# Products of a tile of ones on TensorE in the opening of an attention and double gated-MLP kernel

## The chip, the cores and the metric

The kernel runs on one core of one Trainium2 chip. The metric is the device time of one execution in microseconds (us); several executions of a kernel are timed and their median is compared. One further execution is taken with the hardware profiler, and all rows below come from that one.

## What is computed

Attention over pooled keys and values, then two gated MLPs, all in float32:

```
k_p, v_p = mean of k, v over groups of 8 positions        # 576 -> 72 positions, 4 batches, 8 heads, 64 wide
attn = softmax(q @ k_p.T / 8);  x = attn @ v_p            # x: 2304 tokens x 512
xn = x / sqrt(mean(x*x) + 1e-6) * rms_g
x  = (silu(xn @ w_gate) * (xn @ w_val)) @ w_out           # 512 -> 1536 -> 512
y  = ((x @ w_a) * (x @ w_b)) @ w_out2                     # 512 -> 1536 -> 512
```

The weights arrive as 64-bit floats, so each 128x512 block is loaded as raw words and converted on the chip.

## The kernel before, in words

The work goes through the tokens in tiles of 512, 256, 512, 512 and 512 for the first MLP (`TILES1`), then through the second MLP in slices of 768. Attention is computed in units of 256 tokens, each of two halves of 128. Only the opening matters here: the attention of the first two units, the normalisation of their rows, and the first tile of the first MLP beside the conversion of the weights.

The steps of a unit `u` are small functions. `score_steps` (L288) makes `Au.0` to `Au.9`. Of them `Au.0` and `Au.5` transpose a half of q on TensorE (L298) and copy it out on ScalarE (L307), which frees the buffer of q and lets the next load of q be issued on the SP queue (L283). `Au.1`, `Au.2`, `Au.6` and `Au.7` multiply it with the pooled keys (L318), and VectorE takes the maximum and subtracts it (L327, L328). `Au.3`, `Au.4`, `Au.8` and `Au.9` are the exponential on ScalarE and the division by the row sums. `value_steps` (L358) makes `Vu.0` to `Vu.7`: transposes of the weights of attention (L367), their copies (L374), products with the values (L420), sums of squares with a matrix of ones (L434), a narrow reciprocal square root on VectorE in Newton steps (L478 to L493), a diagonal matrix of the roots (L464), the spread of these roots over all partitions by a product with ones (`spread`, L472), and the scaling (L529). For units 0 and 1 each float32 product shows as two instructions in the trace.

What comes before the scores: k is loaded and pooled on VectorE and GpSimd, transposed (`t0`, L210), and copied into `KB` by ScalarE for one half and VectorE for the other (L220, L222). `ones` (L118) is a 128x128 tile filled by VectorE at the start.

The order of the opening is a list of tokens written by hand, `FIRST` (L32 to L48). `first_tile` hands each to `token` (L763), which runs the named step. After an `@` stand the tags of the PSUM banks that the step takes, in place of the common two. A token with `-` or `=` is put behind the last step without a prefix, on ScalarE, VectorE and GpSimd (`run`, L703); on TensorE no instruction is held in this way, since no step without a prefix is remembered for it. Within that, the framework's scheduler lays out each engine's queue at compile time, from the order of the tokens and from its own model of when an operand is ready. On the chip each queue is worked off in that fixed order, and semaphores make an instruction wait for its operands. `g0a`, `v0a` and so on are halves of the products of the first MLP (L799), `o0` the product with its output weights (L670), `c` the conversion of a block of weights (L589, L590 on ScalarE, L596, L599 on VectorE, L606 on GpSimd), `s0.0` the split of a block into a high and a low part (L620, L621).

```
FIRST = """
=k0 -A0.0@att =k1 l -k2! k3 -l t0@att =A0.1@acc1 A0.2@att w0 =A0.5@acc0 =A0.6@acc3 =A0.7@acc3
-w1 A0.3 =A0.4 w2 t1 =A0.8 A1.0@att A1.1@acc0 A0.9! =c l =A1.2@v -V0.0@acc0 A1.5@acc2 -A1.3
...
```

Of the kernel before, what the change touches and what calls it, by code (L numbers as in the profile page):

```python
# [8 lines left out]
F32 = mybir.dt.float32  # L9
# [8 lines left out]
P = 128  # L18
# [11 lines left out]


FIRST = """  # L32
=k0 -A0.0@att =k1 l -k2! k3 -l t0@att =A0.1@acc1 A0.2@att w0 =A0.5@acc0 =A0.6@acc3 =A0.7@acc3
-w1 A0.3 =A0.4 w2 t1 =A0.8 A1.0@att A1.1@acc0 A0.9! =c l =A1.2@v -V0.0@acc0 A1.5@acc2 -A1.3
-V0.1@acc1 c A1.6@acc3 s0.0 -V0.2@acc0,v A1.4! -V0.3@g,acc0 =A1.7@acc1 A1.8 A1.9 V0.4@acc2,att
=V0.5@att -c =V1.0@acc0 =V0.6 =V0.7@v =V1.1@g -x0! -g0a V1.2@att,acc3 =V1.3@acc2,acc1 c =g0b
-V1.4@acc0,att =l V1.5@acc2 =V1.6 =V1.7@acc0 s0.1! =c =x1 -a0 s1.0 =v0a =v0b -c =h0 =o0 -g1a
-g1b -s1.1! =c L0 -a1 A2.0 -g2a v1a =L1 -g2b p0 =p1! v1b =c s2.0! h1 =c =a2 =c g3a =c v2a =v2b
-h2 =c g3b =o1 a3 =p2 =o2 -v3a =v3b -s2.1 -h3 g4a g4b p3! -c a4 -v4a s3.0 =c -p4 -v4b s3.1! =c
=o3 =g5a =p5! =c =h4 c -c s4.0! -g5b -c -a5 s4.1! v5a -s5.0 v5b -h5 -g6a -o4 -g6b a6 -p6 -c  # L40
=v6a p7 -s5.1 =v6b -A2.1 -g7a -c =g7b -h6 =c =M0 -c =A2.2 =c -A2.3 =s6.1! =s6.0! -a7 o5 -c v7a
=c =A2.4 v7b s7.0! -h7 -g8a -g8b =a8 -o6 s7.1! c =v8a A2.5 c =s8.0 =p8 v8b =g9a -V2.0 g9b -h8
-a9 -o7 v9a =g10a -s9.0 v9b -c =s8.1 -h9 =c =V2.1 =o8 -V2.2 g10b =s9.1! -a10 -c V2.3 =v10a
-V2.4 -c v10b s10.0 g11a -g11b -h10 =a11 =V2.5 =c -s10.1 =c =o9 -g12a =c -v11a s11.0 =A3.0
=g12b -v11b h11 =a12 -V2.6 -v12a =s12.0 -g13a c -o10 A3.1 -v12b -o11 =g13b -s11.1 -s12.1!
=A3.2 -A3.3 =M1 -h12 a13 -v13a -V2.7 -v13b =o12 -h13 =A3.4 =o13 =A3.5
""".split()
SECOND = """  # L48
A4.0 =r0 -r1 r2 -r3 r4 -r5 V3.0 r7 =r6 =r8 -V3.1 =V3.2 N0 =V3.3 A4.1 -N1
# [14 lines left out]
def attention_moe_moe2(  # L64
# [14 lines left out]
    nc = tc.nc  # L79
# [29 lines left out]
    ps = first.enter_context(tc.tile_pool(name="ps", bufs=1, space=bass.MemoryType.PSUM))  # L109
# [7 lines left out]
    ones = const.tile([P, P], F32R, tag="ones", name="ones")  # L117
# [24 lines left out]
    def att_bank(name, tag=None):  # L142
        if tag is not None:
            pass
        else:
            tag = boot["banks"].pop(0) if boot["banks"] else "att"
        return ps.tile([P, 512], F32, tag=tag, name=name, bufs=2 if tag == "att" else 1)
# [210 lines left out]
    def value_steps(u, dest):  # L358
        t0, n = u * UNIT, UNIT
# [109 lines left out]
        def spread():  # L469
            if "diag" in box:  # L470
                bank = att_bank(f"rb_{u}")
                nc.tensor.matmul(  # L472
                    bank[:, :n], ones.bitcast(F32), box["diag"], start=True, stop=True
                )
                box["r"] = bank[:, :n]
# [50 lines left out]
        def scale():  # L526
            xf = dest()
            spread()
            nc.vector.tensor_mul(xf, xf, box["r"].unsqueeze(1).to_broadcast([P, KD, n]))  # L529
# [191 lines left out]
    PE = mybir.EngineType.PE  # L721
    HELD = (PE, mybir.EngineType.Activation, mybir.EngineType.DVE, mybir.EngineType.Pool)
    names = {}

    def name(key, steps):
        for i, st in enumerate(steps):
            names[f"{key}{i}"] = st

    x0 = []

    def split_half(h):
# [17 lines left out]
    name("x", [lambda h=h: split_half(h) for h in range(2)])  # L749
    name("N", loads[3])  # L750
    names["."] = lambda: None
    for u in range(5):
        name(f"A{u}.", A[u])
        name(f"V{u}.", V[u])
# [560 lines left out]
```

## Time and profile before

| | us |
|---|---|
| median of 3 executions | 1023.58 (1022.65 to 1023.66) |
| the profiled execution, its own time | 1024.57 |
| its span, first to last instruction | 1022.8 |
| mean granted TensorE clock over the span | 0.985 of full |

How to read it: times in the rows are microseconds from the start of the span, unless marked ns. PE is TensorE's matmul, PEld its weight load, DVE VectorE, ACT ScalarE, POOL GpSimd, SP the queue that issues the transfers. L298 is line 298 of the kernel before. A group of matmuls that follow each other closely has a start and a length; neighbouring matmuls overlap in the record, so the distance between starts tells the rate, and the length of one tells its latency. The granted clock is the share of full speed that the throttle gave TensorE: 1.00 is 2.4 GHz and 0.50 is 1.2 GHz.

### The profile page before, as it was taken

What the parts mean: (1) busy time and instruction counts of PE and PEld (TensorE: products, weight loads), DVE (VectorE), ACT (ScalarE), POOL (GpSimd) and SP (SyncE); (2) the same over time, 40 slices, a digit from 0 to 9 for tenths busy, and PEclk for the clock granted to TensorE, in tenths of its full rate; (3) what the DMA queues carried; (4) which work ended last, traced back from release to release, by engine and by line L of the source; (5) the groups of instructions that cost most, each with busy time, mean ns of one, the idle gap of its engine ahead of it and who ended that gap; (6) DMA issues with size and microseconds to landing.
All of it is one profiled execution on the core that took longest, in us unless ns stands there. A gap on an engine that the chain in (4) does not pass through costs nothing.

```text
span 1022.8 us, 13568 instructions
## 1 busy us (share of the span) xinstructions
PE 980.8 (96%) x4920; PEld 845.7 (83%) x4920; DVE 612.5 (60%) x966; ACT 451.7 (44%) x848; POOL 399.6 (39%) x324
## 2 busy tenths in 40 slices
PE   4988999999999989999999999999999999999998
PEld 3776676788888877888788899999999999888886
DVE  6898966775634764463628759766776665222221
ACT  3845662454535445444445445444444434321211
POOL 6476672533343433343348611533344333310000
PEclk9889999999999999999999999999999999999999
DMA  8556544320100001000111133443444345643431
GB/s 228 156 175 195 176 141 107 113 70 1 42 8 14 1 6 57 1 1 1 42 44 60 42 115 128 125 160 119 148 146 127 126 137 183 193 136 124 140 115 67
DMA packets 82802, 101.55 MB, mean 99 GB/s; under 512 B 24112, under 2 KB 63024, under 8 KB 82736
## 3 DMA queue, kind: packets, MB, share of 16 engines
q1 hardware_dynamic: 82736, 100.69, 31.7%
q8 instruction: 39, 0.64, 0.3%
q14 instruction: 27, 0.22, 0.1%
HBM read 73.93 MB, written 26.74 MB: 98 GB/s over the span
## 4 chain that ended last, share of the span: by engine, by line
PE 81%; DVE 12%; DMA 3%; issue 2%; ACT 1%; SPq 0%; DVEq 0%; ACTq 0%
PE o L1120 15%; PE X L1019 14%; PE v L649 10%; PE g L649 10%; PE acc L662 9%; PE Y L1019 7%; PE acc L670 4%; PE Z L1019 3%; PE xT L399 2%; PE g L799 2%; PE v L799 2%; PE sc L318 1%; DVE wf L596 1%; DVE wf L599 1%; DMA kv<-in_k_dram 1%
## 5 line engine op out<-in xcount | busy, mean ns | idle before, releaser
L621 POOL TENSOR_TENSOR wl<-wf,wh 128x512 fp32r<-128x512 f32 x144 | 193.6, 1351 | 242.6 <-ACT wh L620 230.3
L620 ACT CAST wh<-wf 128x512 fp32r<-128x512 f32 x156 | 94.9, 618 | 77.9 <-PE v L649 31.8
L1098 DVE TENSOR_TENSOR hl<-hf,hh 128x768 fp32r<-128x768 f32 x36 | 34.3, 958 | 95.5 <-ACT hh L1097 95.4
L1120 PE MATMUL o<-woh,hl 128*128 128x512 f32 x216 | 85.8, 397 | 0.0
L1120 PE MATMUL o<-woh,hh 128*128 128x512 f32 x216 | 85.0, 393 | 0.0
L1120 PE MATMUL o<-wol,hh 128*128 128x512 f32 x216 | 84.7, 392 | 0.0
L606 POOL TENSOR_TENSOR w<-w,st 128x512 int32<-128x512 int32 x24 | 31.9, 1328 | 115.8 <-DVE w L599 114.6
L649 PE MATMUL v<-xh,wl 128*128 128x512 f32 (+1 forms) x192 | 72.7, 379 | 1.8 <-DVE ht L1241 1.8
L649 PE MATMUL g<-xh,wl 128*128 128x512 f32 (+1 forms) x192 | 73.0, 380 | 0.0
L649 PE MATMUL g<-xh,wh 128*128 128x512 f32 (+1 forms) x192 | 70.2, 366 | 0.0
L649 PE MATMUL g<-xl,wh 128*128 128x512 f32 (+1 forms) x192 | 70.2, 366 | 0.0
L649 PE MATMUL v<-xl,wh 128*128 128x512 f32 (+1 forms) x192 | 69.9, 364 | 0.0
L649 PE MATMUL v<-xh,wh 128*128 128x512 f32 (+1 forms) x192 | 69.7, 363 | 0.0
L1097 ACT CAST hh<-hf 128x768 fp32r<-128x768 f32 x36 | 29.8, 834 | 89.8 <-PE o L1120 83.0
L670 PE MATMUL acc<-ht,wf 128*128 128x256 f32 (+1 forms) x208 | 67.5, 466 | 1.2 <-DVE ht L813 0.7
L606 POOL TENSOR_TENSOR wf<-wf,st 128x512 int32<-128x512 int32 x36 | 52.9, 1476 | 39.0 <-DVE wf L599 17.3
L1241 DVE TENSOR_TENSOR ht<-ht,v 128x512 f32<-128x512 f32 (+1 forms) x48 | 29.6, 617 | 64.1 <-PE v L649 60.0
L662 PE MATMUL acc<-hh,wl 128*128 128x512 f32 x144 | 57.5, 399 | 3.8 <-ACT hh L1250 3.8
L1233 ACT ACTIVATE ht<-g 128x512 f32<-128x512 f32 (+1 forms) x48 | 26.1, 544 | 77.8 <-PE g L649 71.7
L662 PE MATMUL acc<-hl,wh 128*128 128x512 f32 x144 | 57.0, 396 | 0.1
L1027 ACT COPY p<-X 128x384 f32<-128x384 f32 x36 | 17.2, 478 | 90.2 <-PE X L1019 90.2
L662 PE MATMUL acc<-hh,wh 128*128 128x512 f32 x144 | 56.8, 394 | 0.0
(208 smaller groups left out, 2713.2 us busy)
## 6 DMA issues: line engine op xcount, KB each, us to landing
hf<-h SPq DMA_DIRECT2D x36, 384.0 KB
st<-in_moe_w_out_dram SPq DMA_DIRECT2D x24, 512.0 KB
h<-u SPq DMA_DIRECT2D x36, 192.0 KB
h<-p SPq DMA_DIRECT2D x36, 192.0 KB
st<-in_moe_w_gate_dram SPq DMA_DIRECT2D x12, 512.0 KB
st<-in_moe_w_val_dram SPq DMA_DIRECT2D x12, 512.0 KB
st<-in_moe_w_a_dram SPq DMA_DIRECT2D x12, 512.0 KB
st<-in_moe_w_b_dram SPq DMA_DIRECT2D x12, 512.0 KB
```

Source lines behind the costliest of these rows:

```text
L606: nc.gpsimd.tensor_tensor(out=bits, in0=bits, in1=low, op=ALU.add)
L620: nc.scalar.copy(wh, wf[ph, f, i])
L621: (nc.vector if boot["alt"] else nc.gpsimd).tensor_sub(wl, wf[ph, f, i], wh.bitcast(F32))
L649: nc.tensor.matmul(bank[:, :n], w[:, c, :], x[:, c, cols], start=(i == 0), stop=(i == 3 * KD - 1),)
L662: nc.tensor.matmul(accs[c][:, cols], w[:, c, :], x[:, :n], start=(f == 0 and i == 0 and cols.start == 0), stop=(f == NF - 1 and i == 2),)
L670: nc.tensor.matmul(accs[c][:, cols], wf[0, f, 2][:, c, :], ht[:, :cols.stop - cols.start], start=(f == 0 and cols.start == 0), stop=(f == ...
L799: nc.tensor.matmul(bank[:, :n], w[:, c, :], x[:, c, cols], start=(c == 0 and i == 0), stop=(c == KD - 1 and i == len(terms) - 1),)
L1019: nc.tensor.matmul(dst[:, :HALF], w[:, c0 + c, :], x[:, c, :], start=(start and i == 0), stop=(stop and i == 5), skip_group_check=True,)
L1097: nc.scalar.copy(hh, hf)
L1098: nc.vector.tensor_sub(hl, hf, hh.bitcast(F32))
L1120: nc.tensor.matmul(accs[i], x[:, sub], y, start=(f == 0 and j == 0), stop=(f == NF - 1 and j == 2),)
L1241: nc.vector.tensor_mul(ht[:, :m], ht[:, :m], vb[:, :m])
```

## The change

Forty-eight products are added, of `ones` with `ones` repeated four times, 128x512 each, in the type fp32r (one instruction and one weight load each). Nothing reads what they write. Each has an ordering edge behind the last TensorE instruction traced before it, with no semaphore; nothing is put behind them by such an edge. They stand in three places:

- `z`, the first token: 24 products, with no TensorE instruction ahead of them.
- `y`: 2 products each behind `A0.0`, `A0.1`, `A0.2`, `A0.5`, `A0.6`, `A0.7`, `A1.0` and `A1.1`, 16 in all. `z` and `y` write one bank with the tag `g`, whose next user is the step `V0.3`.
- `spread` of units 0 and 1: 4 products each, into the bank that the spread itself then writes.

No step of the kernel is removed or moved in the list, and no transfer is added. The diff, with the rest of `FIRST`, which is only wrapped anew, left out:

```
+z =k0 -A0.0@att y =k1 l -k2! k3 -l t0@att =A0.1@acc1 y A0.2@att y w0 =A0.5@acc0 y =A0.6@acc3 y
+=A0.7@acc3 y -w1 A0.3 =A0.4 w2 t1 =A0.8 A1.0@att y A1.1@acc0 y A0.9! =c l =A1.2@v -V0.0@acc0
...
                 bank = att_bank(f"rb_{u}")
+                if u < 2:
+                    keep_busy(4, bank)
                 nc.tensor.matmul(
                     bank[:, :n], ones.bitcast(F32), box["diag"], start=True, stop=True
                 )
...
+    busy = {}
+
+    def keep_busy(count, bank=None):
+
+        before = [i for i in nc.cur_bb.bb.instructions if i.engine == PE]
+        if bank is None:
+            if not busy:
+                busy["bank"] = ps.tile([P, 512], F32, tag="g", name="busy")
+            bank = busy["bank"]
+        for _ in range(count):
+            ins = nc.tensor.matmul(
+                bank, ones, ones.unsqueeze(1).to_broadcast([P, 4, P]), start=True, stop=True
+            ).ins
+            if before:
+                tc.add_manual_dep(
+                    ins, before[-1].name,
+                    mybir.DependencyInfo(mybir.DependencyClass.NoSync, mybir.DependencyReason.DATA),
+                    reason="behind",
+                )
...
+    names["z"] = lambda: keep_busy(24)
+    names["y"] = lambda: keep_busy(2)
```

## Rows read from the trace of the kernel before

**Rows 1.** The page, busy time and share of the span of each engine.

```profile
PE 980.8 (96%) x4920; PEld 845.7 (83%) x4920; DVE 612.5 (60%) x966; ACT 451.7 (44%) x848; POOL 399.6 (39%) x324
```

**Rows 2.** Chain that ended last, 10 to 36 us: start, us, what.

```profile
13.06 2.27 PE sc L318 x8
...
15.81 0.73 DVE e L328 x2
...
24.33 0.90 PE eT L367 x3
25.23 0.96 PE sc L318 x4
26.19 0.43 PE eT L367 x2
26.62 1.71 PE xT L420 x4
...
29.12 0.86 PE xT L420 x4
...
34.14 0.47 PE sq L434 x4
```

**Rows 3.** TensorE in order of time, opening: start, length, [idle before, what ended it].

```profile
10.44 1.09 PE L298 MATMUL qT<-ident,q 128*128 128x128 f32 x4 [10.44 <-DMA q<-in_q_dram]
11.32 0.69 PE L210 MATMUL kT<-ident,kp 72*128 72x72 f32 x4
...
13.06 2.75 PE L318 MATMUL sc<-KB,qTs 128*128 128x144 f32 x12 [0.20 <-DVE KB L222]
...
17.55 0.73 PE L318 MATMUL sc<-KB,qTs 128*128 128x144 f32 x4 [1.04 <-DVE e L328]
...
40.75 0.60 PE L298 MATMUL qT<-ident,q 128*128 128x128 f32 x4
```

**Rows 4.** Busy us (instructions) of PE, PEld, DVE, ACT, POOL; granted clock; DMA share, GB/s.

```profile
22.00:28.80 6.80, 5.77 (x21) 5.03 (x22) 6.47 (x15) 3.15 (x9) 4.43 (x5) 0.50 0.73 227
42.40:49.30 6.90, 5.53 (x23) 4.92 (x23) 5.73 (x15) 6.03 (x12) 2.53 (x3) 0.51 0.76 201
56.10:62.90 6.80, 6.29 (x27) 5.81 (x27) 5.23 (x5) 1.52 (x3) 5.55 (x6) 0.50 0.61 195
10.40:15.00 4.60, 4.36 (x20) 3.99 (x21) 1.92 (x4) 1.53 (x3) 2.31 (x4) 1.00 1.11 318
...
30.00:35.00 5.00, 5.00 (x35) 4.01 (x36) 4.34 (x10) 4.57 (x13) 0.94 (x2) 1.00 0.19 63
...
70.00:80.00 10.00, 8.57 (x44) 7.11 (x43) 9.93 (x13) 5.99 (x10) 8.63 (x7) 1.00 0.77 247
```

**Rows 5.** TensorE in order of time: fp32r products at either clock.

```profile
47.02 0.41 PE L799 MATMUL g<-xh,wh 128*128 128x256 f32 x1
47.23 0.41 PE L799 MATMUL g<-xl,wh 128*128 128x256 f32 x1
...
300.02 0.39 PE L649 MATMUL v<-xh,wh 128*128 128x512 f32 x1
300.24 0.39 PE L649 MATMUL v<-xl,wh 128*128 128x512 f32 x1
```

**Rows 6.** VectorE in order of time: the fill of ones.

```profile
0.88 0.17 DVE L118 MEMSET ones<- 128x128 f32 x1 [0.88 <-PEq L1293]
```

**Rows 7.** TensorE's waits, 32 to 62 us: us in total, times, longest.

```profile
PE rb L472 <- DVE dg L464: 0.9, 1, 0.9
...
PE rb L472 <- DVE dg L464: 2.0, 1, 2.0
PE kT L210 <- DVE kp L189: 1.1, 1, 1.1
```

**Rows 8.** VectorE's waits, 45 to 64 us.

```profile
DVE ht L813 <- PE v L799: 1.6, 1, 1.6
```

More of the change, by code (lines that the diff above doesn't have):

```diff
@@ L32 @@
 FIRST = """
[L33 to L44, printed above, removed]
@@ L45 @@
-=g12b -v11b h11 =a12 -V2.6 -v12a =s12.0 -g13a c -o10 A3.1 -v12b -o11 =g13b -s11.1 -s12.1!
-=A3.2 -A3.3 =M1 -h12 a13 -v13a -V2.7 -v13b =o12 -h13 =A3.4 =o13 =A3.5
+z =k0 -A0.0@att y =k1 l -k2! k3 -l t0@att =A0.1@acc1 y A0.2@att y w0 =A0.5@acc0 y =A0.6@acc3 y
+=A0.7@acc3 y -w1 A0.3 =A0.4 w2 t1 =A0.8 A1.0@att y A1.1@acc0 y A0.9! =c l =A1.2@v -V0.0@acc0
+A1.5@acc2 -A1.3 -V0.1@acc1 c A1.6@acc3 s0.0 -V0.2@acc0,v A1.4! -V0.3@g,acc0 =A1.7@acc1 A1.8
+A1.9 V0.4@acc2,att =V0.5@att -c =V1.0@acc0 =V0.6 =V0.7@v =V1.1@g -x0! -g0a V1.2@att,acc3
@@ new lines @@
+=V1.3@acc2,acc1 c =g0b -V1.4@acc0,att =l V1.5@acc2 =V1.6 =V1.7@acc0 s0.1! =c =x1 -a0 s1.0 =v0a
+=v0b -c =h0 =o0 -g1a -g1b -s1.1! =c L0 -a1 A2.0 -g2a v1a =L1 -g2b p0 =p1! v1b =c s2.0! h1 =c
+=a2 =c g3a =c v2a =v2b -h2 =c g3b =o1 a3 =p2 =o2 -v3a =v3b -s2.1 -h3 g4a g4b p3! -c a4 -v4a
+s3.0 =c -p4 -v4b s3.1! =c =o3 =g5a =p5! =c =h4 c -c s4.0! -g5b -c -a5 s4.1! v5a -s5.0 v5b -h5
+-g6a -o4 -g6b a6 -p6 -c =v6a p7 -s5.1 =v6b -A2.1 -g7a -c =g7b -h6 =c =M0 -c =A2.2 =c -A2.3
+=s6.1! =s6.0! -a7 o5 -c v7a =c =A2.4 v7b s7.0! -h7 -g8a -g8b =a8 -o6 s7.1! c =v8a A2.5 c =s8.0
@@ L47 @@
+=p8 v8b =g9a -V2.0 g9b -h8 -a9 -o7 v9a =g10a -s9.0 v9b -c =s8.1 -h9 =c =V2.1 =o8 -V2.2 g10b
+=s9.1! -a10 -c V2.3 =v10a -V2.4 -c v10b s10.0 g11a -g11b -h10 =a11 =V2.5 =c -s10.1 =c =o9
+-g12a =c -v11a s11.0 =A3.0 =g12b -v11b h11 =a12 -V2.6 -v12a =s12.0 -g13a c -o10 A3.1 -v12b
+-o11 =g13b -s11.1 -s12.1! =A3.2 -A3.3 =M1 -h12 a13 -v13a -V2.7 -v13b =o12 -h13 =A3.4 =o13
+=A3.5
 """.split()
```

## The prediction

> **What bounds the kernel now.** I first read the page's busy shares. TensorE is busy for 96% of the span and no other engine for more than 60% [rows 1], so over most of the kernel only TensorE's work or its speed counts. The opening is where it is not fed, and there I read the chain of waits, then TensorE in order of time, then the stretches with their clock.
>
> The chain runs through TensorE in two places. The first is 13.06 to 15.33, eight score products that VectorE waits for; the second is 24.33 to 34.6, transposes, scores and value products one behind the other with hardly a gap [rows 2]. In between, from 15.8 on, it is mostly VectorE. TensorE does nothing before 10.44, when q has landed [rows 3].
>
> Then the speed. Three stretches of 6.8 to 6.9 us run at a granted clock of 0.50, which is 1.2 GHz: 22.0 to 28.8, 42.4 to 49.3 and 56.1 to 62.9. The table gives 1.00 for 10.4 to 15 [rows 4]. The lengths of the instructions speak against that last figure: four transposes of q take 1.09 us at 10.44 and 0.60 at 40.75, and the first twelve score products take 2.75 where a group of four takes 0.73 at 17.55 [rows 3]. So I take the first burst to have run at the lower of the two clocks, up to about 15, with nothing recorded before the first change. The Trainium skill, "TensorE: Matmul & The Clock Gate" (What's actually happening), says that the throttled state is where the engine starts and that activity releases it, and its caveat under Seeing it yourself says not to trust single records of the clock; the lengths agree with it, the column does not. By the column the first part of the sum below would be a small loss, not a gain; that is a rival.
>
> **The price of one product.** At full clock fp32r products of 512 columns start 0.22 us apart, say 0.23 with its neighbours. At the low clock those of 256 columns start 0.21 apart [rows 5], so one of 512 takes about 0.43, an estimate by twice the columns.
>
> **z, 24 products.** They can start when the ones are filled, at 1.05 [rows 6], and wait for nothing else. The low clock lasted 6.8 us in the stretches that the table shows [rows 4] and about 4.6 in the first burst. If it rises 4.6 to 6.8 us after z starts, 11 to 16 products run at 0.43 and the rest at 0.23, and z ends at 1.05 + 11 x 0.43 + 13 x 0.23 = 8.8 or at 1.05 + 16 x 0.43 + 8 x 0.23 = 9.8. Both lie before 10.44: z costs nothing, its cover being the wait for q. Without a rise it ends at 1.05 + 24 x 0.43 = 11.4, 0.9 late.
>
> **y, and the first scores at full clock.** The four transposes of q fall from 1.09 to 0.60, so their copy starts 0.49 earlier. Two products, 0.46, then stand ahead of the transposes of k. Those started at 11.32 and ended at 12.01 [rows 3]; now they start at 10.88 + 0.46 = 11.34, and with half their spacing end at about 11.75. KB's two copies move with that, and the scores start about 0.3 earlier, at 12.76. Eight of them took 2.27 [rows 2]. Now the first four take 0.56 at 0.14 a start, a pair of 0.46 stands behind them, and the second four are done 0.73 after their start, as at 17.55: 12.76 + 0.56 + 0.46 + 0.73 = 14.5 instead of 15.33. So VectorE's two subtractions at 15.81 [rows 2] come about **0.8** earlier. The other six pairs stand behind a transpose or a score whose reader is ScalarE or VectorE; VectorE is the fuller engine there, so I price them at nothing, and at 0.46 each for those that would stand on the chain (two at most, 0.9). The pairs hold no queue but TensorE's. On SP the loads of q that wait for a transpose are issued up to 0.5 earlier, and nothing is issued later than before except behind a delayed transpose, by up to 0.46.
>
> Of the 0.8 I carry **0.7** to 24.33. The bounds are 0, if transfers or GpSimd set the pace there, and 0.8; with the two pairs on the chain after all, -0.2 is left.
>
> **22.0 to 28.8.** TensorE is busy for 5.77 of 6.8 us here [rows 4]. The four links on the chain from 24.33 take 0.90, 0.96, 0.43 and 1.71, in all 4.00 [rows 2]. At full clock the value products take 0.86, as they do at 29.12 [rows 2]. Scores at 0.14 a start take 0.56 for four, and five transposes at 0.11 take 0.55. That is 1.97 in place of 4.00, so at most 2.0 is to be had. ScalarE must copy the transposes in between, and from 30 to 35 it is busy for 4.57 of 5 us [rows 4], so it is late next. I take **1.5**. Whether the clock holds is unknown: the pairs end behind the first score of the third half, near 19, and the thin stretch after that has only what it had. The bounds are 0, if the clock falls where it fell, and 2.0. I take the upper side, since the stretch before 22 gets four products, 0.9 us of work, and what follows moves forward.
>
> **The fours ahead of the spreads.** They depend on nothing but their place behind the last TensorE instruction traced, so I expect the scheduler to put them well ahead of the spread: in the dense run near 34.5 for unit 0, after the sums of squares near 43.5 for unit 1. Each four costs 4 x 0.23 = 0.9, or 1.7 at the low clock. Their cover is TensorE's idle time of 0.9 ahead of the first spread, and of 1.1 at the transpose of k near 45 ahead of the 2.0 of the second spread [rows 7]. I price them at 0, with bounds of +0.9 (the cover moved away) and, if they keep the clock up in the last low stretch, a gain of up to 1.6: that is what VectorE waits for one value product, v, in that stretch [rows 8]. In 42.4 to 49.3 ScalarE and VectorE are busy for 6.03 and 5.73 of 6.9 us [rows 4], so a faster TensorE there brings nothing.
>
> **The sum.** -0.7 - 1.5 + 0 = -2.2. After 64 us everything follows from conversions and transfers that were themselves released by work of the opening, so I let the 2.2 stand until the end. The profiled execution took 1024.57, 1.0 above the median of 1023.58; it would become 1022.4, and the median **1021.4**. A measurement of this kernel can tell about 0.2% from no change, here 2.05 us, so 1021.53 and 1025.63 are the limits of "the same"; the forecast lies just past the lower one.
>
> **The rivals.**
> - *The last low stretch goes too.* The 1.6 comes on top: 1019.8. For it speak the fours; against it that they may stand 10 us before that stretch. Chance 0.16.
> - *The clock falls near 22 as before, or, as the column has it, the first burst was already fast.* In the first case only the 0.7 is won: 1022.9. In the second the two pairs on the chain cost 0.9 and the 1.5 is won: 1023.0. The long transposes speak against the second. Chance 0.21, of which 0.04 for the column.
> - *It is taken up.* VectorE is busy for 9.93 of 10 us from 70 to 80 [rows 4], where the weights are converted as they land, and what comes earlier waits there; or the scheduler sinks the products to places where they hold nothing up and keep nothing fast, which is the change not doing what it says. 1023.6, chance 0.08.
> - *Slower.* The products stand strictly in TensorE's queue. If the clock is low at 10.44 all the same, because z left it low or because the idle time between z and q let it fall, then the pairs ahead of the first two score groups cost 0.86 each in place of 0.46 and nothing gets faster: 0.9 ahead of the transpose of k, 0.9 behind the second transpose of q and 0.9 between the groups, 2.6 in all: 1026.2. It decides at the first transposes: a length over 0.4 us each. For it speaks that 0.6 to 1.6 us of idle time lie ahead of 10.44; against it that an idle 1.04 us ahead of 17.55 [rows 3] was followed by fast scores. Chance 0.15.
>
> **How the numbers follow.** The forecast has 0.40, with a range of its own from 1020.5 to 1022.7. Of it 0.31 lies below 1021.53; with the first rival's 0.16 that makes faster 0.47. The rest of it, 0.09, with 0.21 and 0.08 makes the same 0.38. Slower is 0.15. The range reaches from 1019.0 (both low stretches gone, less what ScalarE holds back) to 1025.6; beyond it lie most of the slower case and a rest below, 2 in 10.
>
> **What would show it.** Right: the first four transposes take about 0.6 us, the first maximum comes near 13.5 and the subtractions near 15.0; the granted clock is 1.00 from 22 to 28.8; the last sums of squares of unit 0 end near 32.4 instead of 34.6. Wrong: z ends after q has landed; the transposes still take over 1 us; the clock falls near 21 or 25; the spreads start later against the diagonals; or the gain seen at 34 is gone by 90, where VectorE and the loads set the pace.

## The result and the profile after

The kernel became slower. Its median is **1037.19 us** (4 executions, 1036.27 to 1038.78) against 1023.62 for the kernel before beside it: a ratio of 1.0131, interval 1.0114 to 1.0148, some 13.6 us. The profiled execution took 1038.09. The forecast was 1021.4 with a range up to 1025.6, so both its sign and its range were wrong.

The span of that execution is 1036.4 us, against 1022.8 before. The page after, busy time and share of the span of each engine:

```profile
PE 993.1 (96%) x4968; PEld 853.3 (82%) x4968; DVE 618.7 (60%) x966; ACT 452.0 (44%) x848; POOL 401.1 (39%) x324
```

The shares are those of [rows 1]: nothing here shows where 13.6 us went. The table of stretches of after does. (Line numbers differ from kernel to kernel; the names of the tiles do not.) Its columns are the stretch and its length, then busy time and instructions by engine, the granted clock, the transfers' share and GB/s:

```profile
10.40:15.00 4.60, 4.14 (x20) 3.54 (x21) 2.10 (x4) 1.57 (x3) 2.21 (x3) 0.64 1.11 304
...
40.00:50.00 10.00, 6.04 (x27) 4.01 (x25) 8.51 (x17) 5.07 (x13) 3.93 (x3) 0.79 0.74 212
...
60.00:70.00 10.00, 3.40 (x12) 2.63 (x13) 8.51 (x11) 0.00 (x0) 7.68 (x8) 0.64 0.48 147
```

From 40 to 50 TensorE is busy for 6.04 us of 10 and from 60 to 70 for 3.40, while VectorE is busy for 8.51 in both. TensorE of after in order of time, from those rows that answer to [rows 3] and [rows 7] and the new products (brackets: idle time ahead, and what ended it):

```profile
1.10 7.49 PE L742 MATMUL busy<-ones 128*128 128x512 f32 x24 [1.10 <-DVE ones L119]
10.66 0.63 PE L299 MATMUL qT<-ident,q 128*128 128x128 f32 x4 [2.07 <-POOL kp L184]
...
37.23 1.17 PE L742 MATMUL rb<-ones 128*128 128x512 f32 x4
...
47.26 0.36 PE L211 MATMUL kT<-ident,kp 72*128 72x72 f32 x1 [3.15 <-DVE by L495]
47.95 1.22 PE L475 MATMUL rb<-dg,ones 128*128 128x256 f32 x2 [0.34 <-DVE dg L465]
...
52.23 2.05 PE L742 MATMUL rb<-ones 128*128 128x512 f32 x4
...
68.25 1.22 PE L475 MATMUL rb<-dg,ones 128*128 128x256 f32 x2 [5.05 <-DVE dg L465]
```

The products ahead of q do what was forecast: they end at 8.59 and the first four transposes of q take 0.63, not 1.09 [rows 3]. But the spread of unit 0 comes at 47.95, and that of unit 1 at 68.25; the kernel before has them at 40.21 and 54.73. Ahead of both TensorE waits for VectorE, 3.15 us (at the k transpose just in front of the spread) and 5.05 us. That k transpose stood over 5 us behind the first spread before, at 45.83 for 40.21.

VectorE of after between unit 0's sums and its diagonals (dg), and one step of unit 1's root:

```profile
37.34 0.15 DVE L481 TENSOR_SCALAR ba<-sq 128x4 f32<-128x4 f32 x1
37.45 0.69 DVE L602 SCALAR_TENSOR_TENSOR wf<-st,wf 128x512 int32<-128x512 int32 x1
...
38.13 0.42 DVE L599 TENSOR_SCALAR wf<-wf 128x512 int32<-128x512 int32 x1
38.47 1.27 DVE L488 TENSOR_SCALAR br<-br 128x4 int32<-128x4 int32 x1
39.65 0.68 DVE L602 SCALAR_TENSOR_TENSOR wf<-st,wf 128x512 int32<-128x512 int32 x1
...
40.33 0.41 DVE L599 TENSOR_SCALAR wf<-wf 128x512 int32<-128x512 int32 x1
40.66 1.25 DVE L495 TENSOR_TENSOR by<-by,ba 128x4 f32<-128x4 f32 x1
41.83 0.68 DVE L602 SCALAR_TENSOR_TENSOR wf<-st,wf 128x512 int32<-128x512 int32 x1
...
42.81 1.15 DVE L495 TENSOR_TENSOR by<-by,ba 128x4 f32<-128x4 f32 x1
43.99 1.19 DVE L496 SCALAR_TENSOR_TENSOR br<-by,br 128x4 f32<-128x4 f32 x1
45.10 1.01 DVE L190 TENSOR_REDUCE kp<-kv 72x64 f32<-72x512 f32 x1
...
46.11 1.01 DVE L190 TENSOR_REDUCE kp<-kv 72x64 f32<-72x512 f32 x1
...
47.42 0.48 DVE L465 TENSOR_SCALAR dg<-ident,br 128x128 f32<-128x128 f32 x2
...
61.42 3.96 DVE L495 TENSOR_TENSOR by<-by,ba 128x4 f32<-128x4 f32 x1
...
67.63 0.56 DVE L465 TENSOR_SCALAR dg<-ident,br 128x128 f32<-128x128 f32 x2
```

The same part of VectorE in the kernel before:

```profile
34.63 0.16 DVE L478 TENSOR_SCALAR ba<-sq 128x4 f32<-128x4 f32 x1
34.83 1.11 DVE L481 TENSOR_SCALAR br<-ba 128x4 int32<-128x4 int32 x1
...
36.65 0.42 DVE L596 TENSOR_SCALAR wf<-wf 128x512 int32<-128x512 int32 x1
...
37.11 0.69 DVE L599 SCALAR_TENSOR_TENSOR wf<-st,wf 128x512 int32<-128x512 int32 x1
...
38.10 1.14 DVE L491 TENSOR_TENSOR by<-br 128x4 f32<-128x4 f32 x1
...
39.67 0.48 DVE L464 TENSOR_SCALAR dg<-ident,br 128x128 f32<-128x128 f32 x2
```

From the first step of the root to dg it is 10.08 us after and 5.04 before. The 5.04 more can be counted from one start to the next: five instructions of conversions stand among the steps where two did (2.5 for 0.95, so 1.5), two reduces of k (1.9), and four steps hold VectorE for over 1.1 where two did, though their usual length is 0.16 (4.6 for 2.3, so 2.3); the short steps, eight for ten, take 0.7 less. Why a step on 128x4 elements takes over a microsecond, GpSimd of after shows:

```profile
38.28 1.43 POOL L609 TENSOR_TENSOR wf<-wf,st 128x512 int32<-128x512 int32 x1 [6.26 <-DVE br L484]
40.46 1.42 POOL L609 TENSOR_TENSOR wf<-wf,st 128x512 int32<-128x512 int32 x1 [0.76 <-DVE by L494]
42.64 1.29 POOL L609 TENSOR_TENSOR wf<-wf,st 128x512 int32<-128x512 int32 x1 [0.76 <-ACT wh L623]
43.90 1.26 POOL L624 TENSOR_TENSOR wl<-wf,wh 128x512 fp32r<-128x512 f32 x1
...
62.88 2.48 POOL L624 TENSOR_TENSOR wl<-wf,wh 128x512 fp32r<-128x512 f32 x2
```

Each long step ends with a GpSimd instruction: 39.74 and 39.71, 41.91 and 41.88, 43.96 and 43.93, 45.18 and 45.16; the one of 3.96 ends at 65.38, the two of 2.48 at 65.36. A conversion put among the root's steps therefore costs twice in this trace: its own time, and the GpSimd work behind it (L609 for three of the steps, the split L624 for the fourth), which a small step waits out; the step of 3.96 waits out several in a row. The Trainium skill, "SBUF — State Buffer" (SBUF: two separate sides), says that VectorE and GpSimd share one pair of ports under an exclusive lock, which a VectorE instruction needs if it has two inputs in SBUF or runs in a two-port mode, and that the loser waits for the whole instruction; these ends agree with it.

So the account along the path is: unit 0's sums 2.7 late (37.34 for 34.63), its root 5.0 longer, 1.1 more up to unit 1's sums (52.41 for 43.57), unit 1's root 4.95 longer (15.22 from ba to dg for 10.27): 13.8 at unit 1's diagonals and 13.5 at its spread, where the spans differ by 13.6 at the end. The activations of the first MLP carry it on: 12.0 late at 65, 14.9 at 200, 13.0 from 258.

No line of the change touches VectorE. The two programs compared instruction by instruction, with the 48 products left out, differ in the **order** of their queues: at 201 places of TensorE's (within the first 316), 124 of VectorE's, 65 of ScalarE's, 18 of GpSimd's and 14 of SP's. Whatever stands behind is in the same order.

### The profile page after: what moved, and what is told of

It reads as the page before. It is cut to its first block, busy times and chain, and to the rows that moved or that the text cites. A ratio compares the mean times of both kernels' runs of the same rounds, so it can differ in the third digit from the quotient of the medians.

```text
span 1036.4 us, 13661 instructions
## 1 busy us (share of the span) xinstructions
PE 993.1 (96%) x4968; PEld 853.3 (82%) x4968; DVE 618.7 (60%) x966; ACT 452.0 (44%) x848; POOL 401.1 (39%) x324
## 4 chain that ended last, share of the span: by engine, by line
PE 79%; DVE 12%; DMA 4%; issue 2%; ACT 2%; POOL 1%; SPq 0%; DVEq 0%; ACTq 0%; POOLq 0%
PE o L1145 14%; PE X L1044 13%; PE v L652 10%; PE g L652 10%; PE acc L665 9%; PE Y L1044 6%; PE acc L673 3%; PE Z L1044 3%; PE xT L400 2%; PE g L824 2%; PE sc L319 1%; PE v L824 1%; DMA kv<-in_k_dram 1%; DVE wf L599 1%; DVE kp L190 1%
## 5 line engine op out<-in xcount | busy, mean ns | idle before, releaser
L624 POOL TENSOR_TENSOR wl<-wf,wh 128x512 fp32r<-128x512 f32 x144 | 192.7, 1346 | 244.3 <-ACT wh L623 232.2
L609 POOL TENSOR_TENSOR w<-w,st 128x512 int32<-128x512 int32 x24 | 31.9, 1328 | 116.0 <-DVE w L602 114.8
L609 POOL TENSOR_TENSOR wf<-wf,st 128x512 int32<-128x512 int32 x36 | 55.4, 1546 | 48.7 <-DVE wf L602 26.2
```

Source lines behind the costliest of these rows:

```text
L609: nc.gpsimd.tensor_tensor(out=bits, in0=bits, in1=low, op=ALU.add)
L624: (nc.vector if boot["alt"] else nc.gpsimd).tensor_sub(wl, wf[ph, f, i], wh.bitcast(F32))
```

## The experiments

To part the products from the order, a table writes out each engine's queue and ties every instruction to the one ahead of it. A number counts an engine's instructions in the order in which the kernel's code makes them. Of each queue only the stretch in question is shown, cut at both ends, and words stand for whole queues. On VectorE 44 to 57 is unit 0's root from ba to dg, 63 to 76 unit 1's, 61 and 62, 79 and 80, 83 and 84 are pairs of a conversion (43 is the second half of another), 89 and 90 reduces of k, 58 and 77 the scaling of x by a spread. On TensorE 64 and 101 are the spreads, 276 the k transpose.

```diff
+ORDER = {"PE": [...], "DVE": [...], "Activation": [...], "Pool": [...], "SP": [...]}
...
+    for e, seq in want.items():
+        for p, c in zip(seq, seq[1:]):
+            tc.add_manual_dep(lists[e][c], lists[e][p].name, NO_SYNC, reason="order")
```

**The order alone.** No products; the kernel before with all five queues in after's order.

```diff
-# DVE, as scheduled: 44, 45, 46, 47, 48, 49, 61, 50, 62, 51, 52, 53, 54, 55, 56, 57, 79, 80, 58
+"DVE": 44, 43, 45, 61, 46, 62, 47, 79, 48, 80, 49, 50, 51, 52, 89, 53, 90, 54, 55, 56, 57, 58
```

> The kernel before, without any product, with the queues of all five engines put in the order that they have in the changed kernel (edges without a semaphore between neighbours, over the first 316 TensorE, 172 VectorE, 134 ScalarE, 81 GpSimd and 51 SP instructions, where the two differ). Theory 'order' (the products made the scheduler lay out other queues, and these cost the time): 1035 to 1039, about what the changed kernel takes. Theory 'products' (their own time on TensorE and the clock cost it): 1022.5 to 1025. Half and half: near 1030.

Measured: 1036.79 (4 executions), ratio 1.0119 [1.0095, 1.0142]. The products are not needed for the loss; it is the order. Its root of unit 0 takes 10.09 us (36.51 to 46.60) and its second spread comes at 67.30, nearly after's figures.

**The products alone.** All 48, with the queues of before.

```diff
+    nc.tensor.matmul(bank, ones, ones.unsqueeze(1).to_broadcast([P, 4, P]), start=True, stop=True)
+"DVE": 44, 45, 46, 47, 48, 49, 61, 50, 62, 51, 52, 53, 54, 55, 56, 57, 79, 80, 58
```

> The changed kernel with all 48 products, with every other instruction of all five engines in the order of the kernel before. Theory 'order': at most 1025, and if the prediction's sum holds once the order is kept, 1020.5 to 1022.5. Theory 'products': 1035 to 1039.

Measured: 1022.86 (10 executions), ratio 0.9983 [0.9965, 1.0002]. The same kernel once more, in more rounds:

> The kernel with all 48 products and everything else in before's order, once more (1022.86 over 10 runs before, ratio 0.9983 [0.9965, 1.0002]). If the products by themselves are worth what the clock of the first 50 us gives back, 1.1 to 1.3 at the activations between 50 and 120 us in the first run: 1021.5 to 1023.5, with the interval below 1. If the fall of the clock at later waits eats it: the interval holds 1.

Measured: 1023.91 (12 executions), ratio 0.9999 [0.9989, 1.0010]. By themselves the products bring nothing that can be measured, though the clock is what the forecast hoped for and more. The stretches of the products alone:

```profile
22.00:28.80 6.80, 4.79 (x31) 3.83 (x30) 6.73 (x14) 4.45 (x12) 4.82 (x5) 1.00 0.85 249
...
40.00:50.00 10.00, 7.68 (x52) 6.51 (x51) 9.15 (x19) 9.27 (x17) 4.00 (x3) 1.00 0.64 191
```

VectorE of the products alone, with one row of TensorE, says where the gain of the front ends:

```profile
15.27 0.81 DVE L339 TENSOR_TENSOR e<-sc,m 128x288 f32<-128x288 f32 x2
...
21.64 0.84 DVE L351 TENSOR_SCALAR sum<-sum 128x8 f32<-128x8 f32 x1
22.39 0.41 DVE L609 TENSOR_SCALAR wf<-wf 128x512 int32<-128x512 int32 x1
...
28.24 0.20 DVE L352 RECIPROCAL sum<-sum 128x8 f32<-128x8 f32 x1
...
33.10 1.18 PE L752 MATMUL rb<-ones 128*128 128x512 f32 x4
33.34 0.69 DVE L612 SCALAR_TENSOR_TENSOR wf<-st,wf 128x512 int32<-128x512 int32 x1
34.77 0.16 DVE L491 TENSOR_SCALAR ba<-sq 128x4 f32<-128x4 f32 x1 [0.74 <-PE sq L445]
```

In before the same steps stand at 15.73, 22.38, 22.45, 28.30 and 34.63. The gain is 0.46 at the subtractions and 0.74 at the sum's scaling (L351); there that step, usually 0.16, takes 0.84 beside a GpSimd instruction, and from the conversion on the two kernels run alike up to 28.3, at full clock in the one and at half in the other. VectorE is busy for 6.73 of 6.8 us. Behind 28.3 the products alone are 0.46 ahead once more (the conversion at 33.34 stands at 33.80 in before), and the four products ahead of unit 0's spread take that back: they stand at 33.10 for 1.18, in front of the last sums of squares, and VectorE waits 0.74 for those.

**Groups of products**, all in before's order. The first alone:

```diff
-"z =k0 -A0.0@att y =k1 l -k2! k3 -l t0@att =A0.1@acc1 y A0.2@att y w0 ..."
+"z =k0 -A0.0@att =k1 l -k2! k3 -l t0@att =A0.1@acc1 A0.2@att w0 ..."
-                if u < 2:
-                    keep_busy(4, bank)
```

> Only the 24 products of z, with every other instruction in the order of the kernel before. Theory 'order': 1022 to 1024, a gain of up to 0.8 if the clock is still up when q lands. Theory 'products': between 1024 and 1030, since half of the products are left.

Measured: 1026.27 (10), ratio 1.0016 [1.0002, 1.0031], outside the 1022 to 1024 of the theory of the order: 24 products in before's order ran 1.7 over before, where all 48 ran 1.7 under it. Why was not found. The same without the table, in the order that the scheduler gives:

```diff
-ORDER = {"PE": [...], "DVE": [...], "Activation": [...], "Pool": [...], "SP": [...]}
```

> Only the 24 products of z, laid out by the scheduler as it likes; some 20 places on TensorE, 14 on VectorE and 6 on ScalarE then differ from the kernel before. Theory 'order': its distance to the run with z in the old order is what these places cost; it may have either sign, within 4. Theory 'products': the same time as that run, within 0.5.

Measured: 1027.44 (10), ratio 1.0021 [1.0004, 1.0037]; the intervals of the two overlap. Even with only 24 products ahead of q the scheduler lays out other queues; unit 0's sums come at 35.57 and its spread at 41.25. The first two groups without the fours:

```diff
-                if u < 2:
-                    keep_busy(4, bank)
```

> The products ahead of the first q and those behind the first two units' score steps, but not the fours ahead of the spreads; every other instruction in before's order. With all 48 it was 1022.86, with those ahead of the first q alone 1026.27, before 1024.6. If the groups behind the scores hold the clock past 25 us: low clock of 21.3 to 28 in the run with the first group alone goes, and unit 0's sums end near 34.7 as with all 48. If the fours ahead of the spreads hold it past 40: here the clock falls again in 40 to 50 and the time is 1024 to 1026. If the fours do nothing: as with all 48, 1021.5 to 1024, and the spread itself about 0.4 earlier.

Measured: 1023.76 (10), ratio 1.0004 [0.9989, 1.0019]. The last two without the first:

```diff
-z =k0 -A0.0@att y =k1 l -k2! k3 -l t0@att =A0.1@acc1 y A0.2@att y w0
+=k0 -A0.0@att y =k1 l -k2! k3 -l t0@att =A0.1@acc1 y A0.2@att y w0
```

> The products behind the scores and ahead of the spreads, without those ahead of the first q; everything else in before's order. In the run with the first group alone (1026.27) the q transposes went from 1.09 to 0.63 and the activations came 0.6 to 1.0 earlier up to 120 us, but the time was longer. If the first group is worth its 0.5 to 0.7 and no more: 0.5 to 0.7 over the run beside it with all 48. If the first group costs something (as it seemed alone): 1 or more under the run beside it. If it does nothing: within 0.4 of it.

Measured: 1027.52 (8), ratio 1.0033 [1.0019, 1.0046]. Here the clock, from 22 to 28.8 and 40 to 50, with the first group alone:

```profile
22.00:28.80 6.80, 5.16 (x22) 4.47 (x21) 6.51 (x13) 3.60 (x10) 4.89 (x5) 0.58 0.75 220
...
40.00:50.00 10.00, 8.62 (x42) 7.79 (x40) 8.72 (x18) 8.59 (x16) 4.05 (x3) 0.56 0.65 187
```

and with the first two:

```profile
22.00:28.80 6.80, 5.07 (x32) 3.87 (x31) 6.77 (x16) 5.14 (x13) 4.40 (x5) 1.00 0.89 246
...
40.00:50.00 10.00, 8.47 (x43) 7.47 (x44) 9.15 (x19) 8.49 (x16) 3.99 (x3) 0.66 0.64 192
```

The pairs behind the scores keep 22 to 28.8 at full clock (0.58, then 1.00), and the fours keep 40 to 50 (0.66, then 1.00 above). Each group does to the clock what it is for. The times don't follow: unit 0's sums come at 33.88 with the first group alone, at the low clock, at 34.38 with two groups and at 34.77 with all. None of the three things expected of the last run was measured: it is 3.6 slower than the kernel with all 48 beside it, where the first group was to be worth 0.7 at most. Why was not settled: its profiled execution took 1024.43, its fastest, while the others took up to 1029.99. The first group alone ran 1.7 over before and the kernel without it 3.1 over, so these runs give no price for a single group.

**Which part of the order.** After's order up to unit 0's sums and before's behind them, then the mirror:

```diff
+"DVE": [after's order of 0 to 43 and 78] + [before's order of the rest]
```

> No products. Each queue has after's order for what stands, in before, ahead of the first step of unit 0's inverse root (on TensorE up to unit 0's last sum of squares), and before's order for all that follows. All of after's order was 1036.79, before 1023.8 to 1024.6. Theory A (the cost lies behind the sums, in the cut-up roots, the spreads behind other work and the products of the second layer): 1024 to 1027, the front only 1 to 2 late at unit 0's sums (36.0 against 34.6 in the run with all of after's order). Theory B (the front sets it: unit 1's softmax and transposes come later, and what follows waits): 1031 or more.

Measured: 1026.73 (10), ratio 1.0026 [1.0017, 1.0036]; the second spread at 57.27.

```diff
+"DVE": [before's order of 0 to 43 and 78] + [after's order of the rest]
```

> No products. The mirror of the run before: before's order up to unit 0's sums, after's order for all that follows. Theory A: 1033 to 1037, the spread of unit 0 behind 44 and that of unit 1 behind 64. Theory B: 1025 to 1029. If the two parts add up, the excesses of both runs over before sum to 12.

Measured: 1034.78 (4), ratio 1.0098 [1.0079, 1.0116]; the spreads at 44.34 and 64.69. Over before (1024.14) that is 2.6 and 10.6, in all 13.2 where the whole order costs 12: most of the cost lies behind the sums. Now by engines: TensorE's and VectorE's queues of after with the other three of before, and the mirror:

```diff
+"PE": after, "DVE": after, "Activation": before, "Pool": before, "SP": before
```

> No products. TensorE's and VectorE's queues in after's order, ScalarE's, GpSimd's and SP's in before's. All of after's order 1036.79, before 1024. Theory A (the two queues that hold the roots, the spreads and the products carry it): 1034 to 1037. Theory B (the DMA issues and the conversions on ScalarE and GpSimd that moved carry it, through late weights): 1024 to 1028.

Measured: 1039.19 (4), ratio 1.0154 [1.0139, 1.0168], 14.8 over before.

```diff
+"PE": before, "DVE": before, "Activation": after, "Pool": after, "SP": after
```

> No products. The mirror: ScalarE's, GpSimd's and SP's queues in after's order, TensorE's and VectorE's in before's. Theory A: 1023 to 1027. Theory B: 1033 or more.

Measured: 1031.24 (4), ratio 1.0072 [1.0059, 1.0085]. The two queues with the roots and spreads are enough for the whole loss, but the mirror fits neither theory: it should have cost 3 at most and costs 6.9. In it TensorE waits 3.86 for GpSimd's division of unit 0's exponentials:

```profile
28.17 0.90 PE L377 MATMUL eT<-ident,e 128*128 128x128 f32 x3 [3.86 <-POOL e L352]
```

The two parts add up to 21.7, not 12. Both mixtures of queues lose, so the loss of the order cannot be shared out among the engines by them.

**Putting pieces back.** After's order with unit 0's root in one piece, and its spread ahead of the k transpose:

```diff
-"DVE": 44, 43, 45, 61, 46, 62, 47, 79, 48, 80, 49, 50, 51, 52, 89, 53, 90, 54, 55, 56, 57, 58
+"DVE": 44, 45, 46, 47, 48, 49, 50, 51, 52, 53, 54, 55, 56, 57, 43, 61, 62, 79, 80, 89, 90, 58
-"PE": 133, 276, 64, 93, 94, 97, 98, 99, 100, 67, 68, 102, 103, 69
+"PE": 133, 64, 93, 94, 97, 98, 99, 100, 67, 68, 102, 103, 276, 69
```

> The kernel before, without products, every queue in after's order, but with two pieces put back: VectorE's steps of unit 0's inverse root (from the first after the unit's sums to the last, dg) stand one behind the other again, and TensorE's spread of unit 0 (rb_0) stands ahead of the second k transpose (kT) and not behind it. The run with all of after's order was 1036.79, before 1024.6. Theory (the root of a unit, cut up between conversions and reduces of k, is what the order costs; unit 0's took 10.5 us there against 5.5 before): at least 5 of the 12 come back at rb_0, some stays for unit 1's root (15.6 us against 11.1), so 1030 to 1032. Rival (VectorE is full in this stretch and the displaced conversions only come later, ahead of something that waits for them): within 1.5 of 1036.8, with rb_0 near 42 but the Silu's drift of +10 at 65 us unchanged.

Measured: 1032.98 (4), ratio 1.0095 [1.0079, 1.0112]. Then unit 1's root in one piece too, from its second step on:

```diff
-"DVE": 64, 86, 65, 87, 66, 88, 67, 91, 68, 92, 69, 85, 70, 71, 72, 73, 74, 75, 76, 77
+"DVE": 64, 65, 66, 67, 68, 69, 70, 71, 72, 73, 74, 75, 76, 86, 87, 88, 91, 92, 85, 77
```

> As the run before, and VectorE's steps of unit 1's inverse root stand one behind the other too. Theory (the cut-up roots are what the order costs): another 3 to 4 come back, 1026 to 1029. Rival (VectorE is full, what is moved comes back later): 1034 or more. If only unit 0's root mattered: no further gain, about as the run before.

Measured: 1031.07 (4), ratio 1.0078 [1.0063, 1.0094]. That is 3.8 and then 1.9 less: the direction of the theory, short of its sizes. Against the kernel before beside each run, the excess goes from 12.2 to 9.2 and 7.3. The trace with both roots together shows what took the rest, on VectorE and on TensorE:

```profile
38.42 0.48 DVE L474 TENSOR_SCALAR dg<-ident,br 128x128 f32<-128x128 f32 x2
...
45.42 1.22 DVE L539 TENSOR_TENSOR xf<-xf,rb 128x1024 f32<-128x1024 f32 x1
...
53.74 0.48 DVE L474 TENSOR_SCALAR dg<-ident,br 128x128 f32<-128x128 f32 x2
...
58.29 2.93 PE L680 MATMUL acc<-ht,wf 128*128 128x256 f32 x6 [2.88 <-DVE ht L823]
61.01 1.06 PE L482 MATMUL rb<-dg,ones 128*128 128x256 f32 x2
```

The root now takes 2.4 us, but its diagonals lie unused: the displaced conversions and reduces stand ahead of xf, and unit 1's spread stands behind products that wait for ht. So the next edit put these behind the path as well:

```diff
-"DVE": 57, 43, 61, 62, 79, 80, 89, 90, 58 ... 76, 86, 87, 88, 91, 92, 85, 77
+"DVE": 57, 43, 61, 58, 62, 79, 80, 89, 90 ... 76, 86, 87, 77, 85, 88, 91, 92
-"PE": 122, 115, 116, 117, 101
+"PE": 122, 101, 115, 116, 117
```

> No products, after's order, with both roots together as in the run at 1031.07, and the path behind the roots put back as well: on VectorE the product of x with the spread (xf) stands two instructions behind dg for both units (in that run unit 0's stood behind seven, conversions and reduces, and began at 45.4 where its spread had come at about 44), the gate's product (ht) behind that of unit 1, and on TensorE unit 1's spread (rb_1) stands ahead of the second layer's products that wait for ht (it came at 61.0 there, 6.8 behind dg). Theory (what is on the path stands behind what is not): 1026 to 1029. Rival (VectorE is full, conversions put behind come late for the products): within 1.5 of 1031.

Measured: 1038.6 (4), ratio 1.0135 [1.0119, 1.0151], 7.5 slower than the run before it instead of 2 to 5 faster: a plain miss of both expectations. Four rows of it, of VectorE, GpSimd, ScalarE and TensorE:

```profile
45.55 1.22 DVE L539 TENSOR_TENSOR xf<-xf,rb 128x1024 f32<-128x1024 f32 x1 [4.95 <-PE rb L482]
...
47.51 1.33 POOL L616 TENSOR_TENSOR wf<-wf,st 128x512 int32<-128x512 int32 x1 [5.77 <-DVE wf L609]
...
48.88 0.62 ACT L630 CAST wh<-wf 128x512 fp32r<-128x512 f32 x1 [6.15 <-POOL wf L616]
...
51.38 2.72 PE L444 MATMUL sq<-ones,sq 128*128 128x2 f32 x12 [5.87 <-ACT sq L435]
```

VectorE waits 4.95 for a spread that stands on TensorE behind unit 1's value products; a conversion waits behind it, GpSimd for that, a cast on ScalarE for GpSimd, and behind the cast the squares of unit 1 that TensorE's sums wait for. What is off the path on one queue releases what is on it on another. So of the 12 us the cut-up roots account for about 5 by these runs; how the other 7 divide over the rest of the order was not shown.

**The roots of before itself.** Unit 1's root in one piece from its second step on, in before's order:

```diff
-"DVE": 63, 89, 64, 90, 59, 60, 65, 83, 66, 86, 67, 84, 68, 87, 69, 88, 70, 71, 85, 72
+"DVE": 63, 89, 64, 65, 66, 67, 68, 69, 70, 71, 72, 73, 74, 75, 76, 90, 59, 60, 83, 86
```

> The kernel before in its own order, without products, but VectorE's steps of unit 1's inverse root, which even in before stand among conversions and reduces (11.1 us from first to dg), put one behind the other. Theory (a cut-up root is time on the path): 2 to 5 faster than before, 1019 to 1022, rb_1 at about 50 for 54.7. Rival (VectorE is full there, the conversions are due themselves): within 1.5 of before, 1023 to 1026, with rb_1 earlier and a later tile later by as much.

Measured: 1026.37 (5), ratio 1.0044 [1.0028, 1.0060]: 2.6 slower, outside both expectations. Its dg comes at 47.27 for 53.84, and the spread at 55.34 for 54.73: the k transpose in front of it now waits 3.46 for a reduce that was put behind the root. Last, all 48 products with unit 0's root in one piece:

```diff
-"DVE": 44, 45, 46, 47, 48, 49, 61, 50, 62, 51, 52, 53, 54, 55, 56, 57, 79, 80
+"DVE": 44, 45, 46, 47, 48, 49, 50, 51, 52, 53, 54, 55, 56, 57, 61, 62, 79, 80
```

> All 48 products in their places, every other instruction in before's order, but VectorE's steps of unit 0's inverse root one behind the other (in before two pairs of a conversion stand among them, 0.42 and 0.69 us each). With the products in before's order it was 1022.86 against 1024.6. Theory: dg about 1.1 earlier, rb_0 at 38.7 for 39.8, and the time 1021 to 1022.5. Rival (as with unit 1's root put together, 1026.37: the conversion that is put behind is itself due): 1023.5 to 1026.

Measured: 1022.56 (10), ratio 0.9991 [0.9976, 1.0006], between the two expectations, the spreads at 38.97 and 53.36. No version was shown to beat the kernel before.

## Why the prediction was wrong

**The step that failed** is in the change part: "The pairs hold no queue but TensorE's." The sum took every other instruction to keep its place. In truth the scheduler lays out all queues together, from its model of when an operand is ready, and 48 products that nothing reads changed 221 places besides TensorE's 201. With the products and before's order the time is 1022.86 and 1023.91, with after's order and no products 1036.79. The sentence of the rivals that the scheduler might sink the products saw the scheduler, but only what it would do to the products.

Point by point, the rest read from the run with the products alone:

- *z ends at 8.8 to 9.8, before q has landed.* Right: 9.37 there, and 8.59 after, a little under the lower bound. Whether it costs nothing is open, since the run with z alone was 1.7 slower.
- *The first burst ran at the lower clock.* Right: with z ahead, four transposes take 0.63 for 1.09, and the column that showed 1.00 for before was wrong.
- *The subtractions come 0.8 earlier.* Half: 0.46.
- *-0.7 carried to 24.33 and -1.5 in 22 to 28.8.* Wrong in size, both near 0. The clock held (1.00), yet VectorE's steps from 22.4 to 28.3 stand where they stood. The chain of waits led through TensorE there [rows 2], and I took its links for the bound; VectorE was busy without a gap beside them and set the pace. [rows 4] had it, 6.47 of 6.80 us, and I quoted only TensorE's 5.77. The bound 0 of the text was the value to take up to 28.3. The sums of squares that were to end near 32.4 ended at 34.73.
- *The fours cost 0, between +0.9 and -1.6.* The place was right without the reordering (33.10 and 42.55, expected near 34.5 and 43.5). They were not free: VectorE waits 0.74 behind them at unit 0's sums, which come 1.43 after the conversion ahead of them, and 0.61 after it in the run without the fours. With after's order they stand at 37.23 and 52.23.
- *The slower rival* had its place at the first transposes, with pairs at the low clock. That did not happen there (0.63 for four). In after the clock did fall behind them, to 0.64 over 10.4 to 15, but the order alone gives the loss without it.

Right apart from the order, then, was the effect on the clock and not its worth: a forecast of -2.2 where the medians of the products alone are -1.7 and -0.5, the second with an interval of about 1 us on either side of nothing.

## What to carry to other kernels

Where a scheduler lays out the queues, an instruction that depends on nothing and is read by nothing is still a change to every queue: compare the instruction order of the two programs engine by engine before costing anything, and hold the old order when only the new work is to be measured. A faster stretch of one engine was worth nothing here where another is busy throughout beside it, even though the chain of waits led through the first. In this kernel conversions between the short steps of the path cost their own time and that of the GpSimd work behind them, but moving those alone moved the wait to another queue.

## What was not expected of the hardware

In the rows above a VectorE step of 0.16 us took 1.11 to 3.96 where it met GpSimd's elementwise work, and ended 0.02 to 0.03 behind it each time; it does so in before as well (34.83, 1.11 us). Not every step was held: the one at 34.63, which reads the sums out of PSUM, took 0.16 beside the same GpSimd instruction (34.62 to 35.91).

Executions of one and the same kernel spread over up to 6.7 us (1020.88 to 1027.61 over the 25 of the kernel before beside the first runs; 1019.65 to 1025.47 with all products, 1021.64 to 1026.90 the second time). In the profiled executions kernels that ran alike for a hundred microseconds moved apart at single waits where the clock fell in one and not in the other: from 250 to 260 the granted clock is 0.83 in before and 1.00 with the products alone, and the activations behind it stand 2.2 earlier instead of 0.7. Whether the spread between executions has this cause was not shown, since each run has one profile.
